# Spectral mixing with a gated feed-forward layer on one core: stores of the gate and up stage issued by GpSimd from the second weight group on

## The chip, the cores and the metric

The kernel runs on one core of one Trainium2 chip. The metric is the device time of one execution in microseconds, the median of several runs. All data is fp32.

## The reference

Two branches work on the same activations x (2 batches of 4096 tokens, width 640) and are mixed by a gate for each token. Cut to what matters:

```python
g = sigmoid((x * gate_w).sum(-1, keepdims=True))

# branch a: a spectral mixer along the 4096 tokens
Xf = rfft2(x, axes=(1, 2))                 # then 4 blocks of 160 channels
hr = relu(zr @ w1[0] - zi @ w1[1] + b1[0]) # complex 2-layer MLP in each block
hi = relu(zi @ w1[0] + zr @ w1[1] + b1[1])
or_, oi_ = ...                             # the same with w2, b2, then soft shrinking by 0.01
a = irfft2(or_ + 1j * oi_, s=(1, 4096))

# branch b: a gated feed-forward layer, hidden width 1728
b = (gelu(x @ w_gate) * (x @ w_up)) @ w_down

out = g * a + (1 - g) * b
```

## The kernel before

The program has three stages that follow each other on TensorE: the gate and up products of branch b (up to about 1380 us), the spectral mixer's middle (up to about 1800 us), and the inverse transform with the down product. The change lies in the first. Every product is made of three matmuls of fp32r parts (high x high, high x low, low x high), and the parts are called forms here: a high part is copied by ScalarE (line 278), the low part subtracted by VectorE (line 281). Products of 2 x 2 blocks are made with seven block products instead of eight, so sums and differences of blocks (t1 to t4 of the activations) get forms too.

**Loops.** The 14 tiles of 128 hidden columns are cut into three weight groups: tiles 0 to 3, 4 to 7 and 8 to 13. For each group the kernel goes over 16 keys, a key being one group and one strip of 512 tokens (two keys make a row couple where a second level of the seven-product scheme joins them: `deep`, strips 3 to 12 in the first two groups). For each key it goes over the group's tiles; one tile of one key is a `quad`. A quad's matmuls are cut into seven steps, and at each step a hook runs what was planned for it: slot 7 x tile + step of that key. `spread(i, s, [f])` plans f for slot s of key i or later. The tables of slots are thus an order written out by hand, and each engine works its instructions in that order.

**Forms of the next key.** `x_prep(nxt, k)` makes form k of the next key: b11, k4, t3, b21, t2, t5, t1, b22, t4 for k = 0 to 8. In the first group t1 to t4 are computed (differences by VectorE, then the form) and kept in device memory by DMAs that GpSimd issues (xD, line 500). From the second group on SyncE loads them instead (line 467), into one of 14 `mid` buffers; the load waits until TensorE has done with what was there.

**Other work in the slots.** From key 14 on the first transform of the spectral mixer runs between quads: `a_load` loads a strip of x (xr, line 790), `a_split` makes its forms xs, `a_step` makes two matmuls a call (line 817) and stores the result as to scr1. In the third group `wd_pre` loads the down weights (draw) and makes seven forms wf for each of seven row pairs, stored in wdf and wdl. In the last key the weights of the spectral MLP are prepared (wm, wl, from raw, rs and rl), partly on GpSimd (lines 884, 885, 904, 912, and line 281 for wm).

**Stores.** A quad ends in h = gelu(gate) * up for 128 hidden columns and 512 tokens, which `h_store` writes to hD, four pieces of 512 bytes for each partition; `half_store` writes half of it. All stores go through `st`, which only lists them; at the end of each quad `flush` issues the listed ones on SyncE's queue, the queue that issues the loads too:

```python
    ld = nc.sync.dma_start
    late = []
    def st(dst, src):
        late.append((dst, src))
    def flush():
        for dst, src in late:
            ld(dst, src)          # line 257
        late.clear()
```

A store waits on SyncE until its source has been made, and what is behind it on that queue waits too. Sources and loaded raw data share 18 `small` buffers; an instruction that takes a buffer next waits until the store that reads it has landed.

The slots of the forms are set here (`z` is 21 in the first two groups, so z + 1, z + 4 and z + 6 are the last of a key's 28 slots; `nxt` is the next key):

```python
            for k, s in enumerate((5, 8, 11, 14, 16, 18, z + 1, z + 4, z + 6) if gr < 2 else
                                  (6, 9, 13, 17, 21, z + 1, z + 2, z + 3, z + 3, z + 5)):
                if k > 5 and deep(key) and not deep(nxt):
                    s += 3
                if k < 9 or nxt[0] == 2:
                    f0, f1, f2_ = x_prep(nxt, k)
                    spread(i, s - 1, [f0])
                    spread(i, s + 1, [f1, f2_])
```

Of the kernel before, what the change touches and what calls it, by code (L numbers as in the profile page):

```python
# [10 lines left out]
F32 = mybir.dt.float32  # L11
# [4 lines left out]
P = 128  # L16
N = 4096
D = 640
# [196 lines left out]
def spectral_mix_kernel(ctx: ExitStack, tc: tile.TileContext, a):  # L215
    nc = tc.nc
    out = a["out"]

    def dr(t, off, ap):
        return bass.AP(tensor=t.tensor, offset=t.offset + off, ap=ap)  # L220
# [7 lines left out]
    def bank():  # L228
        return psum.tile([P, 512], F32, name="bank", tag="bank")
# [13 lines left out]
    def small(shape, dt=F32, name="small"):  # L243
        return pool.tile(shape, dt, name=name, tag="small", bufs=18)
# [6 lines left out]

    def st(dst, src):
        late.append((dst, src))

    def flush():
        for dst, src in late:
            ld(dst, src)
        late.clear()

    scr1 = [dram.tile([32, P, D], F32, name=f"scr1_{b}") for b in range(2)]  # L260
# [3 lines left out]
    hD = dram.tile([64, P, 14 * P], F32, name="hD")  # L264
    wdf = [dram.tile([P, 13 * 320], F32, name=f"wdf_{j}") for j in range(7)]
    wdl = dram.tile([P, 7 * 320], F32, name="wdl")
# [10 lines left out]
    def high(dst, src, scale=1.0):  # L277
        nc.scalar.activation(dst, src, AF.Copy, scale=scale)  # L278
# [4 lines left out]
    def split(dst_h, dst_l, src, eng=nc.vector):  # L283

        high(dst_h, src)
        low(dst_l, src, dst_h, eng)
# [22 lines left out]
    def deep(key):  # L309
        return key[0] < 2 and FIRST <= key[1] < LAST  # L310
# [135 lines left out]
    def x_raw(key, names=("b11", "b21", "b12", "b22", "k4")):  # L446
        d = XT.setdefault(key, {})
        for n in names:
            if (key[0] != 1 or made(key) or n != "b12") and not (key[0] == 1 and deep(key) and n == "b21"):
                r = d[n] = small([P, 512], name="xraw")  # L450
                ld(r, a["xT"][key[1], ("b11", "b21", "b12", "b22", "k4").index(n)])
# [112 lines left out]
                inner.pop()()  # L564

    def h_store(tp, t, h):
        st(dr(hD, 4 * tp * P * 14 * P + t * P, [[14 * P, P], [P * 14 * P, 4], [1, P]]),
           h.rearrange("p (t n) -> p t n", t=4))

    def x_of(o, *names):  # L570
# [11 lines left out]
    def quad(key, t, hook):  # L582
# [65 lines left out]
        def half4():  # L648
            run(C, prod(w["u2"], x_of(o, "t4")), first=False)
            nc.vector.tensor_add(u2, C, u2)  # L650
            nc.vector.tensor_mul(v["h2"], v["h2"], v["u4"])  # L651
            if ahead_:
                half_store(key[1], t, 1, v["h2"])
            elif not dp:
                nc.vector.tensor_mul(v["h"][:, :256], u2, p1)
                h_store(key[1], t, v["h"])
# [18 lines left out]
                q.pop(0)[1]()  # L675

    def half_store(tp, t, q, h):
        st(dr(hD, (4 * tp + 2 * q) * P * 14 * P + t * P, [[14 * P, P], [P * 14 * P, 2], [1, P]]),
           h.rearrange("p (t n) -> p t n", t=2))

    def deep_parts(gr, tp, t):
# [95 lines left out]
    F1, XR, XS, GW = {}, {}, {}, []  # L777
# [28 lines left out]
    def a_step(b, n2, h):  # L806
        xs = XS.pop((b, n2, h))
        m = n2 if n2 < 16 else 32 - n2
        f = F1[m // 5][:, m % 5]
        if h == 0:  # L810
            XS[b, n2] = small([P, D], name="as")
        stg = XS[b, n2]
        hi, lo = (slice(0, 64), slice(64, P))[::1 - 2 * h]
        for q in range(2):
            cs = slice(320 * q, 320 * q + 320)
            pa = bank()
            nc.tensor.matmul(pa[:, :320], f[:, h], xs[:, cs], start=True, stop=True)  # L817
            nc.scalar.activation(stg[hi, cs], pa[lo, :320], AF.Copy)  # L818
            nc.vector.tensor_add(stg[hi, cs], pa[hi, :320], stg[hi, cs])  # L819
        if h:  # L820
            st(dr(scr1[b], n2 * D, [[32 * D, 4], [P * D, 32], [1, D]]), XS.pop((b, n2)))

    def gates(b):
        nc.scalar.activation(gs[:, b, 0], G[:, b], AF.Sigmoid)
# [357 lines left out]
    def wd_raw(t):  # L1182
        raw = RAW["d", t] = small([P, D], name="draw")
        if t < NPAIR:
            ld(raw, a["wd"][t * P:(t + 1) * P])
        else:
            nc.gpsimd.memset(raw[64:], 0.0)
            ld(raw[:64], a["wd"][t * P:])
# [10 lines left out]
    def wd_pre(j):  # L1199
        o = {}  # L1200
        pair = (j, j + 6) if j < 6 else (12, 13)

        def loads():
            for t in pair:
                wd_raw(t)

        def sums(k):
            def f():
                if not o:
                    r1, r2 = (RAW.pop(("d", t)) for t in pair)  # L1210
                    o.update(b11=r1[:, :320], b12=r1[:, 320:], b21=r2[:, :320], b22=r2[:, 320:])
                n, p, q = (("t1", "b12", "b11"), ("t2", "b22", "t1"), ("t3", "b22", "b12"), ("t4", "b21", "t2"))[k]
                if k % 2 == 0:
                    o["x"] = small([P, 2, 320], name="wx")
                o[n] = o["x"][:, k % 2]
                nc.vector.tensor_sub(o[n], o[p], o[q])
            return f

        def form(n):
            def f():  # L1220
                w = small([P, 2, 320], F32R, name="wf")
                p, q = HI[n], LO.get(n, 13)
                wh, wl = (w[:, 0], w[:, 1]) if p < q else (w[:, 1], w[:, 0])
                if j == 6 and n in HALF:
                    x = o[n][:64]
                    nc.gpsimd.memset(wl[64:].bitcast(F32), 0.0)
                    split(wh[:64], wl[:64], x)
                    high(wh[64:], x)
                else:
                    split(wh, wl, o[n])  # L1230
                if n == "b22":
                    st(dr(wdf[j], 320 * p, [[13 * 320, P], [1, 320]]), wh.bitcast(F32))
                    st(dr(wdl, 320 * j, [[7 * 320, P], [1, 320]]), wl.bitcast(F32))
                else:
                    st(dr(wdf[j], 320 * min(p, q), [[13 * 320, P], [320 * abs(q - p), 2], [1, 320]]), w.bitcast(F32))
            return f
        return [loads], [sums(0), sums(1), form("t1"), form("b21")], [sums(2), sums(3), form("t2"), form("b11"),
                                                                      form("t3"), form("t4"), form("b22")]
# [308 lines left out]
    def spread(i, s, fs):  # L1547

        for k, f in enumerate(fs):
            j, q = i, max(s + k, 0)  # L1550
            while j < last and q >= points(j):
                j, q = j + 1, q - points(j)
            slots.setdefault((j, q), []).append(f)
# [6 lines left out]
    for k, (b, n2) in enumerate(a_seq):  # L1560
        i, j = steps_a[k]
# [16 lines left out]
    for i, (gr, tp) in enumerate(keys):  # L1578
        if deep((gr, tp)) and tp % 2:
            p, f = x_deep(gr, tp)  # L1580
# [26 lines left out]
            spread(34 + 2 * j, 1 + 5 * k, [f])  # L1607
    for i, key in enumerate(keys):
        gr, tp = key
        nxt = keys[i + 1] if i < last else None  # L1610
        quads = [t for t in groups[gr] if t < NPAIR]
        nq = len(quads)
        if nxt:
            if not i:
                x_raw(nxt)
            z = 7 * (nq - 1)
            for k, s in enumerate((5, 8, 11, 14, 16, 18, z + 1, z + 4, z + 6) if gr < 2 else
                                  (6, 9, 13, 17, 21, z + 1, z + 2, z + 3, z + 3, z + 5)):
                if k > 5 and deep(key) and not deep(nxt):
                    s += 3  # L1620
                if k < 9 or nxt[0] == 2:
                    f0, f1, f2_ = x_prep(nxt, k)
                    spread(i, s - 1, [f0])
                    spread(i, s + 1, [f1, f2_])
            if gr < 2 and nxt[0] == 2:
                spread(i, z + 7, x_prep(nxt, 9))
        for j, t in enumerate(quads):
            def hook(k):
                for f in slots.get((i, 7 * j + k), ()):
                    f()  # L1630
            (quad if i else plain)(key, t, hook)
            if gr == 2 and j == 1:
                mixed(key)
            if i % 16 == 15:
                WG.pop(t)
            if 0 < i + 1 < last and j == nq - 1:
                x_raw(keys[i + 2])
            n = len(late)
            for f, *args in todo.get((i, j), []):
                f(*args)  # L1640
            new = late[n:]
            del late[n:]
            flush()
            late.extend(new)
        for q in range(7 * nq, 7 * nq + 14) if i == last else ():
            for f in slots.get((i, q), ()):
                f()
        XO.pop(key)
# [13 lines left out]
    for ch in range(1, 2 * NCH):  # L1662
        b, c = chunks[ch]
# [9 lines left out]
    wl = lambda part, *js: [(wd_load, j, part) for j in js]  # L1673
# [13 lines left out]
    for i in range(S + 2):  # L1687
# [18 lines left out]
        if 0 <= i - 1 < S:  # L1706
            b, c, n = steps[i - 1]
# [72 lines left out]
```

## Time and profile before

| | |
|---|---|
| three runs | 2531.83, 2541.38, 2542.81 us; median 2541.38 |
| profiled execution | 2531.49 us, its span 2529.7 us |
| TensorE matmuls, weight loads | busy 2522.0 and 2516.3 us |
| VectorE, ScalarE, GpSimd | busy 2078.9, 1492.6 and 387.3 us |
| SyncE's DMA queue | 445.02 MB, 54.6% of the 16 DMA engines' span |
| GpSimd's DMA queue | 51.00 MB, 5.5% of it |

The span runs from the first to the last instruction; the execution's own time is 1.8 us longer. Rows of the profile name the engine (PE is TensorE, PEld its weight loads, DVE VectorE, ACT ScalarE, POOL GpSimd, SP SyncE; a q marks the queue that issues), the source line, the operation and output<-input without buffer numbers. In a timeline the first column is the start and the second the duration, both in us; in square brackets stands how long the engine was idle before it and what ended that. In a list of waits the numbers are microseconds in total, times, and the longest.

### The profile page before, as it was taken

To read this page: it belongs to the slowest core of one execution; us is meant where nothing else is said; L and a number is where in the kernel's file an instruction comes from. 1 tells how busy PE (TensorE), PEld (TensorE's weight loads), DVE (VectorE), ACT (ScalarE), POOL (GpSimd) and SP (SyncE) were. 2 spreads that over 40 slices of the span, in tenths; PEclk is the share of its full clock that TensorE was granted. 3 is DMA by queue.
4 is the path that set the end of the run, shared out by engine and by line. 5 is a ranking of instruction groups with operands and counts; after the bars stand their busy time and mean duration, and the time that the engine had idled before them with its cause. 6 is when DMAs were issued, how large, how long until landed. Compare 5 with 4: busy or idle time off the path is not lost.

```text
span 2529.7 us, 54653 instructions
## 1 busy us (share of the span) xinstructions
PE 2522.0 (100%) x20239; PEld 2516.3 (99%) x20239; DVE 2078.9 (82%) x4323; ACT 1492.6 (59%) x3503; POOL 387.3 (15%) x404
## 2 busy tenths in 40 slices
PE   9999999999999999999999999999999999999999
PEld 9999999999999999999999999999999999999999
DVE  7677788777777877787668788888999999899998
ACT  5455456656656666666556778787644444444443
POOL 0111100000000000000003111111133333333332
PEclk9999999999999999999999999999999999999999
DMA  6566666777777677777667455548744444444432
GB/s 216 203 214 229 224 224 211 245 234 241 234 251 236 220 235 243 237 239 227 217 228 220 130 164 142 161 144 270 289 142 147 157 157 140 133 152 157 154 131 102
DMA packets 351422, 499.50 MB, mean 197 GB/s; under 512 B 26028, under 2 KB 223276, under 8 KB 351156
## 3 DMA queue, kind: packets, MB, share of 16 engines
q1 hardware_dynamic: 333684, 445.02, 54.6%
q0 software_dynamic: 17472, 51.00, 5.5%
q8 instruction: 159, 2.61, 0.4%
q14 instruction: 107, 0.88, 0.1%
HBM read 307.10 MB, written 188.81 MB: 196 GB/s over the span
## 4 chain that ended last, share of the span: by engine, by line
PE 95%; DVE 2%; DMA 2%; ACT 1%; issue 0%; SPq 0%; DVEq 0%; ACTq 0%
PE bank L562 52%; PE bank L1406 22%; PE bank L297 14%; PE bank L983 3%; PE bank L694 2%; PE bank L817 1%; PE bank L1064 1%; PE bank L1065 1%; DMA xraw<-in_xT_dram 0%; DMA wdf<-wf 0%; PE bank L1066 0%; DMA scr<-as 0%; DMA zl<-zl 0%; DVE xo L281 0%; DMA wx<-wdf 0%
## 5 line engine op out<-in xcount | busy, mean ns | idle before, releaser
L562 PE MATMUL bank<-xo,w 128*128 128x256 f32 x11196 | 1319.4, 277 | 1.6 <-ACT u L588 0.6
L562 PEld LDWEIGHTS bank<-xo,w 128*128 128x128 f32 x11196 | 1298.0, 188 | 3.4 <-ACT u L588 1.2
L1406 PE MATMUL bank<-wx,ho 128*128 128x320 f32 x3844 | 560.7, 306 | 0.0
L1406 PEld LDWEIGHTS bank<-wx,ho 128*128 128x128 f32 x3844 | 557.2, 187 | 0.0
L281 DVE TENSOR_TENSOR ho<-hraw,ho 128x640 fp32r<-128x640 f32 (+3 forms) x384 | 260.8, 720 | 23.1 <-ACT ho L278 20.2
L588 ACT ACTIVATE u<-bank 128x256 f32<-128x256 f32 x328 | 125.5, 383 | 174.6 <-PE bank L562 166.4
L278 ACT ACTIVATE ho<-hraw 128x640 fp32r<-128x640 f32 x320 | 167.1, 571 | 97.7 <-PE bank L1406 74.9
L281 DVE TENSOR_TENSOR xs<-xr,xs 64x640 fp32r<-64x640 f32 x128 | 105.0, 820 | 75.8 <-ACT xs L278 73.6
L640 DVE TENSOR_TENSOR u<-bank,u 128x256 f32<-128x256 f32 x204 | 85.9, 421 | 86.4 <-ACT u L588 85.5
L281 DVE TENSOR_TENSOR xo<-xraw,xo 128x512 fp32r<-128x512 f32 x194 | 133.2, 687 | 16.4 <-ACT xo L278 15.1
L297 PE MATMUL bank<-wm,h 128*128 128x320 f32 (+1 forms) x792 | 137.6, 309 | 0.0
L819 DVE TENSOR_TENSOR as<-bank,as 64x320 f32<-64x320 f32 x256 | 113.9, 484 | 21.8 <-ACT as L818 20.1
L278 ACT ACTIVATE xo<-xraw 128x512 fp32r<-128x512 f32 x194 | 121.6, 627 | 6.1 <-DMA xraw<-in_xT_dram 4.9
L297 PEld LDWEIGHTS bank<-wm,h 128*128 128x128 f32 (+1 forms) x792 | 117.9, 185 | 1.3
L588 ACT ACTIVATE p<-bank 128x256 f32<-128x256 f32 x144 | 55.2, 383 | 105.8 <-DVE h L651 54.6
L562 PE MATMUL bank<-wx,ho 128*128 128x320 f32 x764 | 116.3, 307 | 0.0
L562 PEld LDWEIGHTS bank<-wx,ho 128*128 128x128 f32 x764 | 112.0, 188 | 0.0
L818 ACT ACTIVATE as<-bank 64x320 f32<-64x320 f32 x256 | 96.7, 426 | 23.8 <-PE bank L817 20.3
L278 ACT ACTIVATE xs<-xr 64x640 fp32r<-64x640 f32 x128 | 94.0, 734 | 22.9 <-DMA xr<-in_x_dram 21.1
L278 ACT ACTIVATE ho<-hs 128x640 fp32r<-128x640 f32 (+1 forms) x128 | 68.5, 570 | 61.5 <-DVE ho L281 42.1
L770 POOL MEMSET h<- 64x512 f32 x16 | 8.4, 523 | 624.9 <-PE bank L817 249.1
L1373 ACT ACTIVATE uu<-bank,gs 128x320 f32<-128x320 f32 x120 | 54.7, 524 | 76.5 <-PE bank L297 76.0
(196 smaller groups left out, 3961.8 us busy)
## 6 DMA issues: line engine op xcount, KB each, us to landing
xo<-xD SPq DMA_DIRECT2D x124, 512.0 KB
xraw<-in_xT_dram SPq DMA_DIRECT2D x215, 256.0 KB
hD<-h SPq DMA_DIRECT2D x184, 256.0 KB
hraw<-hD SPq DMA_DIRECT2D x128, 320.0 KB
xD<-xo POOLq DMA_DIRECT2D x64, 512.0 KB, 3.6
sc<-scr SPq DMA_DIRECT2D x65, 320.0 KB
xr<-in_x_dram SPq DMA_DIRECT2D x64, 320.0 KB
scr<-as SPq DMA_DIRECT2D x64, 320.0 KB
```

The costliest lines, as they stand in the source:

```text
L278: nc.scalar.activation(dst, src, AF.Copy, scale=scale)
L281: eng.tensor_sub(dst, src, hi.bitcast(F32))
L297: nc.tensor.matmul(dst, l, r, start=i == 0, stop=i == len(ops) - 1)
L562: nc.tensor.matmul(dst, l, r, start=first and i == 0, stop=i == len(ops) - 1, skip_group_check=True)
L588: copy = lambda d, s_: nc.scalar.activation(d, s_, AF.Copy)
L640: nc.vector.tensor_add(u4, C, u4)
L694: nc.tensor.matmul(acc, l, r, start=first and i == 0, stop=i == 2, skip_group_check=True)
L818: nc.scalar.activation(stg[hi, cs], pa[lo, :320], AF.Copy)
L819: nc.vector.tensor_add(stg[hi, cs], pa[hi, :320], stg[hi, cs])
L983: nc.tensor.matmul(pz[:, kp * P:(kp + 1) * P], SC[b, c, kp][:, o:o + P], ft, start=True, stop=True)
L1373: nc.scalar.activation(uu[n2][:, cs], pe[:, :320], AF.Copy, scale=gs[:, b, 0, n2:n2 + 1])
L1406: nc.tensor.matmul((X, Y)[k], *op, start=n[k] == 0 and not (more and k), stop=n[k] == tot[k] - 1, skip_group_check=True)
```

## The change

From the second weight group on, `h_store`, `half_store`, `a_step` and the weight forms of `wd_pre` call `st_g` instead of `st`. It issues the store at once on GpSimd's queue, at the place where it is called, and no longer at the quad's end on SyncE's. In the first group they go through `st` as before, and so do the stores of the later stages that call `st`. Second, where a key is `deep` and the next one isn't (strip 12 of the first two groups), form k = 4 (t2 of the next key) moves by seven slots, from 16 to 23; forms 6 to 8 are moved by three there as before.

```diff
+    group = [0]
+
+    def st_g(dst, src):
+        if group[0]:
+            nc.gpsimd.dma_start(dst, src)
+        else:
+            st(dst, src)
+
     def h_store(tp, t, h):
-        st(dr(hD, 4 * tp * P * 14 * P + t * P, [[14 * P, P], [P * 14 * P, 4], [1, P]]),
+        st_g(dr(hD, 4 * tp * P * 14 * P + t * P, [[14 * P, P], [P * 14 * P, 4], [1, P]]),
            h.rearrange("p (t n) -> p t n", t=4))
...
         if h:
-            st(dr(scr1[b], n2 * D, [[32 * D, 4], [P * D, 32], [1, D]]), XS.pop((b, n2)))
+            st_g(dr(scr1[b], n2 * D, [[32 * D, 4], [P * D, 32], [1, D]]), XS.pop((b, n2)))
...
                 if n == "b22":
-                    st(dr(wdf[j], 320 * p, [[13 * 320, P], [1, 320]]), wh.bitcast(F32))
-                    st(dr(wdl, 320 * j, [[7 * 320, P], [1, 320]]), wl.bitcast(F32))
+                    st_g(dr(wdf[j], 320 * p, [[13 * 320, P], [1, 320]]), wh.bitcast(F32))
+                    st_g(dr(wdl, 320 * j, [[7 * 320, P], [1, 320]]), wl.bitcast(F32))
...
     for i, key in enumerate(keys):
         gr, tp = key
+        group[0] = gr
...
-                if k > 5 and deep(key) and not deep(nxt):
-                    s += 3
+                if deep(key) and not deep(nxt):
+                    s += {4: 7, 6: 3, 7: 3, 8: 3}.get(k, 0)
```

(`half_store` and the other branch of the weight forms change in the same way.) Eight lines are added above the quads, so line 257 becomes 259, 467 becomes 475, and so on.

SyncE's queue at a couple's end in the second group, before. xo is a form of the next key loaded from xD_13, xr a strip for the first transform, hD, scr1 stores:

```order
L790 DMA xr_10315<-in_x_dram 128x640
L524 DMA xs_10329<-xA_11_117 128x512
L257 DMA hD_104<-h2_10337 128x2x128
L467 DMA xo_10405<-xD_13_101 128x1024
L257 DMA scr1_1_69<-as_10339 4x32x640
L467 DMA xo_10470<-xD_13_101 128x1024
L790 DMA xr_10528<-in_x_dram 128x640
L257 DMA hD_104<-pb_9908 128x2x128
L467 DMA xo_10584<-xD_13_101 128x1024
L451 DMA xraw_10626<-in_xT_dram 128x512
```

The same place now:

```order
L798 DMA xr_10315<-in_x_dram 128x640
L532 DMA xs_10329<-xA_11_117 128x512
L475 DMA xo_10406<-xD_13_101 128x1024
L798 DMA xr_10527<-in_x_dram 128x640
L475 DMA xo_10567<-xD_13_101 128x1024
L475 DMA xo_10584<-xD_13_101 128x1024
L459 DMA xraw_10628<-in_xT_dram 128x512
```

The three stores are gone from between the loads, and the second xo, which is t2, stands behind the xr load instead of ahead of it.

GpSimd's queue in the last key, where it prepares the spectral weights, before (raw, wl: weights; zl2: a constant part of a later operand):

```order
L884 TENSOR_TENSOR raw_19616<-raw_19616 128x128
L885 TENSOR_TENSOR raw_19616<-raw_19616 128x128
L950 MEMSET zl2_19808 64x1024
L951 MEMSET zl2_19808 2x1024
L950 MEMSET zl2_19811 64x1024
L951 MEMSET zl2_19811 2x1024
L904 MEMSET wl_19840 64x2x256
L912 TENSOR_TENSOR wl_19840<-rs_19620,bh_19841 64x2x256
L884 TENSOR_TENSOR raw_19715<-raw_19715 128x128
```

The same place now:

```order
L892 TENSOR_TENSOR raw_19616<-raw_19616 128x128
L893 TENSOR_TENSOR raw_19616<-raw_19616 128x128
L259 DMA hD_104<-h_19780 128x4x128
L958 MEMSET zl2_19809 64x1024
L959 MEMSET zl2_19809 2x1024
L958 MEMSET zl2_19812 64x1024
L959 MEMSET zl2_19812 2x1024
L912 MEMSET wl_19840 64x2x256
L920 TENSOR_TENSOR wl_19840<-rs_19620,bh_19841 64x2x256
L892 TENSOR_TENSOR raw_19715<-raw_19715 128x128
```

A store of h now stands between the first weights and the memsets, so all that follows on GpSimd waits until VectorE has made that h.

GpSimd's queue in the third group, where a couple's weight forms are stored, now (before, GpSimd had nothing here):

```order
L259 DMA hD_104<-h_12673 128x4x128
L259 DMA wdf_0_105<-wf_12713 128x2x320
L259 DMA scr1_0_68<-as_12636 4x32x640
L259 DMA hD_104<-h_12767 128x4x128
L259 DMA wdf_0_105<-wf_12782 128x2x320
L259 DMA scr1_1_69<-as_12798 4x32x640
```

Here six stores that stood on SyncE between loads follow each other, a four-piece h store just ahead of a weight form.

More of the change, by code (lines that the diff above doesn't have):

```diff
@@ L677, in half_store @@
     def half_store(tp, t, q, h):
-        st(dr(hD, (4 * tp + 2 * q) * P * 14 * P + t * P, [[14 * P, P], [P * 14 * P, 2], [1, P]]),
+        st_g(dr(hD, (4 * tp + 2 * q) * P * 14 * P + t * P, [[14 * P, P], [P * 14 * P, 2], [1, P]]),
            h.rearrange("p (t n) -> p t n", t=2))
@@ L1231, in f @@
                 if n == "b22":
-                    st(dr(wdf[j], 320 * p, [[13 * 320, P], [1, 320]]), wh.bitcast(F32))
-                    st(dr(wdl, 320 * j, [[7 * 320, P], [1, 320]]), wl.bitcast(F32))
+                    st_g(dr(wdf[j], 320 * p, [[13 * 320, P], [1, 320]]), wh.bitcast(F32))
+                    st_g(dr(wdl, 320 * j, [[7 * 320, P], [1, 320]]), wl.bitcast(F32))
                 else:
-                    st(dr(wdf[j], 320 * min(p, q), [[13 * 320, P], [320 * abs(q - p), 2], [1, 320]]), w.bitcast(F32))
+                    st_g(dr(wdf[j], 320 * min(p, q), [[13 * 320, P], [320 * abs(q - p), 2], [1, 320]]), w.bitcast(F32))
             return f
```

## The prediction

> **What bounds the kernel now.** I read the page first.
>
> ```profile
> span 2529.7 us, 54653 instructions
> PE 2522.0 (100%) x20239; PEld 2516.3 (99%) x20239; DVE 2078.9 (82%) x4323; ACT 1492.6 (59%) x3503; POOL 387.3 (15%) x404
> PEclk9999999999999999999999999999999999999999
> ```
>
> TensorE is busy for 2522.0 of 2529.7 us, at full clock in every slice. Since a busy TensorE need not be TensorE at its peak, the second view is busy time by stretch. The changed part reaches from the second weight group's start (near 418 us) to the last of the gate and up stage (near 1380 us); the third stretch holds the last row couple's last key, where the next stage is prepared.
>
> ```profile
> core 0: us, PE busy (x) PEld busy (x) DVE busy (x) ACT busy (x) POOL busy (x), PEclk, DMA share, GB/s
> 418.00:800.00 382.00, 381.85 (x3321) 381.06 (x3320) 285.38 (x659) 229.48 (x543) 2.66 (x5) 1.00 0.73 237
> 800.00:1340.00 540.00, 539.60 (x4702) 539.41 (x4702) 405.04 (x918) 340.37 (x803) 11.60 (x23) 1.00 0.73 232
> 1340.00:1380.00 40.00, 39.74 (x344) 39.27 (x343) 35.15 (x83) 24.50 (x73) 23.55 (x31) 1.00 0.80 243
> ```
>
> Over these 962 us TensorE's matmuls are idle for 0.15 + 0.40 + 0.26 = 0.81 us, and its weight loads for 0.94 + 0.59 + 0.73 = 2.26 us. The matmul count per microsecond is the same in the first two stretches (3321 / 382 = 8.69 and 4702 / 540 = 8.71), so no slow feeding hides inside the busy time. **So whatever the change improves here, this execution can give back 0.8 us, and 2.3 us at most.** GpSimd is nearly free until 1340 us (14 of 922 us) and 59% busy after it.
>
> Third, the waits of SyncE's queue and of ScalarE between 410 and 1340 us:
>
> ```profile
> SPq L257 <- DVE h L655: 165.3, 60, 6.7
> SPq L467 <- PE bank L562: 26.8, 40, 8.3
> ACT xs L278 <- DMA xr<-in_x_dram: 21.1, 13, 4.1
> ```
>
> SyncE stands 165 us in 60 stores (line 257) until VectorE has made the h that they store, and the loads queue behind them. ScalarE in turn waits 21 us for xr loads. The longest such wait, in time:
>
> ```profile
> 1136.86 1.05 SPq L790 DMA_DIRECT2D xr<-in_x_dram  x1
> 1143.91 0.74 ACT L278 ACTIVATE xs<-xr 64x640 fp32r<-64x640 f32 x1 [4.07 <-DMA xr<-in_x_dram]
> 1144.68 0.82 DVE L281 TENSOR_TENSOR xs<-xr,xs 64x640 fp32r<-64x640 f32 x1 [5.04 <-ACT xs L278]
> PE bank L562 <- DVE u L640: 0.4, 1, 0.4
> ```
>
> An xr load that was issued late held ScalarE for 4.07 and VectorE for 5.04 us, and TensorE felt 0.4 us of it, its only listed wait in this stretch. Elsewhere the cushion was thick enough.
>
> **The change, part by part.** *Stores off SyncE.* 300 stores leave its queue: 141 of h in four pieces a partition, 40 of half an h in two pieces, 63 of as, 56 of weight forms. SyncE isn't the bound, so this is worth only what late loads cost TensorE now: between 0 and the 0.8 us of matmul idle; I take 0.4, the one wait above.
>
> *Stores on GpSimd.* The trace has DMAs issued by GpSimd, all with one contiguous piece a partition:
>
> ```profile
> L500 POOL DMA_DIRECT2D xD<-xo x64: 531/531/699, 24.6 to 455.6; - x64
> DMA to landing us min/median/max: 2.9/3.6/8.2
> ```
>
> No row has two or four pieces. If pieces cost nothing, a store occupies GpSimd for 0.53 us: 300 x 0.53 = 159 us. If its time goes by pieces, it is 2.12 us for four and 1.06 for two; 21 of the weight forms have two: 141 x 2.12 + 61 x 1.06 + 98 x 0.53 = 416 us, 43% of 962. GpSimd doesn't saturate at either end. I take 1.1 us for the large store, nearer the lower end, since that is the only measured row.
>
> What a slow store can delay is the buffer that it reads. In the changed order, the shortest recurring distance from a producer to the instruction that waits for the store's landing is a weight form whose buffer ScalarE's xs takes next:
>
> ```profile
> 872.27 0.49 DVE L281 TENSOR_TENSOR wf<-draw,wf 128x320 fp32r<-128x320 f32 x1
> 872.79 0.36 SPq L257 DMA_DIRECT2D wdf<-wf  x1
> 879.40 0.74 ACT L278 ACTIVATE xs<-xr 64x640 fp32r<-64x640 f32 x1
> ```
>
> From 872.76 to 879.40 are 6.64 us. The store needs 1.1 us of issue (two pieces, upper end) and 3.6 us to land, counted from its issue on: at most 4.7 us, with 1.9 us over. With a four-piece h store just ahead of it, at its upper end, it is 6.8 us, 0.2 us late. I take no cost.
>
> On this a rule speaks against the change: VectorE can lock GpSimd out while it writes descriptors. The row above says 531 ns as minimum and median of 64 issues and 699 as maximum, beside a VectorE that is busy 82% of the span. The Trainium skill, "SBUF — State Buffer", section "SBUF: two separate sides", states that a DMA issued by GpSimd is starved of descriptors while VectorE runs an operation in a two-port mode. By it each store would start up to one VectorE operation (0.5 us) later, and the distance of 6.64 us would still hold, so the sum is the same by both; the trace shows no starving.
>
> *Order on GpSimd in the last key.* This is where I see a price. GpSimd prepares weights there; now it must first issue the store of an h that VectorE makes at 1346.41.
>
> ```profile
> 1346.41 0.42 DVE L655 TENSOR_TENSOR h<-u,p 128x256 f32<-128x256 f32 x1
> 1343.19 0.98 POOL L950 MEMSET zl<- 64x1024 f32 x1
> 1346.25 0.95 POOL L951 MEMSET zl<- 2x1024 f32 x1
> 1348.78 1.40 POOL L912 TENSOR_TENSOR wl<-rs,bh 64x512 fp32r<-64x512 f32 x1 [1.12 <-ACT bh L278]
> 1350.14 0.46 POOL L884 TENSOR_TENSOR raw<-raw 128x128 f32<-128x128 f32 x1
> 1351.40 0.64 POOL L885 TENSOR_TENSOR raw<-raw 128x128 f32<-128x128 f32 x1
> 1352.57 1.88 ACT L278 ACTIVATE wm<-raw 128x128 fp32r<-128x128 f32 x10
> 1356.56 0.59 ACT L771 ACTIVATE gelu<-bank 64x512 f32<-64x512 f32 x1 [2.11 <-issue]
> ```
>
> Four zl memsets run from 1343.19 to 1347.20 now, ahead of that h. After: h at 1346.83, store 0.53 to 2.12, memsets 4.0, the wl memset 0.5 and wl 1.4, four raw operations 1.9 (1350.14 to 1352.04). That ends at 1355.2 to 1356.8 where it ended at 1352.04. ScalarE's ten wm copies need raw and start 2.6 to 4.2 us after 1352.57. Its 2.11 us of idle ahead of L771 absorb that much; it is 0.5 to 2.1 us late for the bank copies that release TensorE. I take 1.0 us; the bounds are 0 (banks ahead cover it) and 4.2 (nothing does).
>
> *The form made later.* At a couple's end t2 of the next key moves by seven steps, one tile.
>
> ```profile
> 712.10 0.52 SPq L257 DMA_DIRECT2D scr<-as  x1
> 721.60 0.32 SPq L467 DMA_DIRECT2D xo<-xD  x1
> 722.02 0.38 SPq L790 DMA_DIRECT2D xr<-in_x_dram  x1
> ```
>
> In the second group this is the load that holds SyncE from 712.62 to 721.60, for a buffer that TensorE still reads, with an xr load behind it. Moved behind that xr load it waits for a buffer still, so it lands about when it did (0.4 us later for one more issue), and xr goes first. In the first group VectorE and ScalarE do the same four instructions one tile later. I take 0, bounds 0.4 either way.
>
> **Sum.** -0.4 + 0 + 1.0 + 0 = +0.6 us on the profiled execution, which took 2531.49 us (span 2529.7): 2532.1, between -2.3 and +4.6.
>
> The three timed runs gave 2531.83, 2541.38 and 2542.81: the profiled execution is like the fastest, and the median lies 9.9 us above. No view shows where the others lost those 10 us. A late xr load, as at 1136.86, is a candidate: its 5 us of VectorE idle nearly reached TensorE. The change gives exactly these loads more lead, so I hold the lower level the likelier for its median. **Forecast: 2532 us**, which is 0.37% under the median before; about 0.5% is what a measurement of this kernel can tell from no change, so it counts as no change.
>
> **The rivals.** *No effect on the level*: 2541.4 + 0.6 = 2542 us, if the 10 us have nothing to do with SyncE's queue. For it: no row ties them to it. Also no change.
>
> *Slower: stores land too late in the third group.* If GpSimd's stores land as its slowest row (8.2 us) and not as the median, the weight form takes 1.1 + 8.2 = 9.3 us against 6.64: ScalarE stands 2.7 us, once a key, in 16 keys, 43 us. ScalarE is idle 37% (200 of 540 us) there, so some 27 us reach TensorE: 2531.5 + 27 = 2559 us, and at the upper level 2568. It decides from a landing of 5.5 us (6.64 less 1.1) on. For it: DMA engines are 73% busy there, and the pieces are small. Against: the median of 64 is 3.6.
>
> *Faster by over 0.5%*: that is under 2528.7 us. All 2.26 us of weight-load idle gone and no price in the last key: 2531.49 - 2.26 = 2529.2, still short by 0.5 us; it takes the start or the other stages as well. That the change does nothing is excluded: 300 stores stand in another queue in the built order.
>
> **Chances.** Forecast at the lower level 0.46, no effect on the level 0.29, slower 0.17, faster 0.08. Same is 0.46 + 0.29 = 0.75. The range reaches from 2528 (2531.49 less the 2.3 bound, and 1 more for the start) to 2552 (the upper level's 2542.8 with the +4.6 bound, 2547, and into the slower case by the first third of its 27 us from 2543); it leaves out most of the slower case and some of the faster, under 0.2.
>
> **What would show it.** Right: TensorE's idle in 418 to 1340 us stays under 0.6 us; SyncE's wait for h is gone from its list; ScalarE's wait for xr falls well under 21 us; GpSimd's hD stores show under 2.2 us each; ScalarE's wm copies near 1352 us start 2 to 4 us later. Wrong: waits of ScalarE or VectorE for "hD<-h" or "wdf<-wf" of more than a few us in sum, GpSimd issues over 2.2 us, or TensorE waits that recur once a key.

## The result and the profile after

The changed kernel takes 2543.61 us in the median of 19 runs (2538.47 to 2559.43), the kernel before 2531.22 us in 19 runs (2529.70 to 2545.62). The ratio is 1.0048, with a 95% interval of 1.0031 to 1.0066: slower, by about 12 us. The forecast was no change, at 2532 us.

Most runs of both kernels and of the variants stand at one of two levels some 12 us apart (before: 14 of 19 near 2530.8, 5 near 2542.8; after: 14 near 2542.7, 5 near 2556.1), so differences below are given at the lower level, against before's runs of the same comparison, of which four far out (2760 to 7905 us) are left aside.

The profiled execution of the changed kernel took 2539.39 us, 7.9 us more than the profiled one of before. First its page, then busy time in the three stretches that the prediction used.

```profile
span 2537.4 us, 54880 instructions
PE 2526.4 (100%) x20239; PEld 2518.8 (99%) x20239; DVE 2080.8 (82%) x4323; ACT 1492.0 (59%) x3503; POOL 602.1 (24%) x704
```

```profile
418.00:800.00 382.00, 381.84 (x3322) 380.99 (x3321) 286.54 (x659) 229.27 (x544) 80.78 (x111) 1.00 0.72 239
800.00:1340.00 540.00, 538.03 (x4663) 536.25 (x4662) 401.98 (x911) 336.29 (x796) 141.26 (x204) 1.00 0.69 229
1340.00:1380.00 40.00, 38.25 (x325) 37.66 (x324) 29.73 (x78) 22.15 (x67) 21.83 (x31) 1.00 0.76 247
```

The matmul counts say where the time went. In the second weight group nothing changed (3322 against 3321). In the third, 39 of 4702 matmuls are missing, 4.5 us at 8.71 a us. Around the last key, up to 1380 us, 19 more are missing, 2.2 us. GpSimd's busy time rose by 215 us and is far from full, as predicted.

The waits of ScalarE for transfers in the third group, of the changed kernel, show what is new:

```profile
ACT xs L286 <- DMA wdf<-wf: 12.8, 5, 3.8
ACT xs L286 <- DMA xr<-in_x_dram: 9.7, 5, 2.5
ACT xo L286 <- DMA xraw<-in_xT_dram: 7.2, 6, 2.2
ACT xs L286 <- DMA hD<-h: 6.4, 4, 2.3
ACT wf L286 <- DMA scr<-as: 3.7, 3, 1.8
ACT h L597 <- DMA scr<-as: 3.3, 3, 1.7
```

The same list of before has two entries:

```profile
ACT xs L278 <- DMA xr<-in_x_dram: 13.8, 8, 4.1
ACT wf L278 <- DMA wdf<-wf: 1.0, 1, 1.0
```

ScalarE now waits some 26 us for stores to land, where it was 1, and 17 us for loads, where it was 14. SyncE, which stood 130 us for h in this stretch before, now stands 246 us at the xo loads until TensorE frees a buffer: the loads run ahead as far as the buffers let them. At the place that the prediction priced at nothing, the timeline of the changed kernel reads:

```profile
872.71 0.71 POOL L259 DMA_DIRECT2D wdf<-wf  x1
873.04 9.17 SPq L459 DMA_DIRECT2D xraw<-in_xT_dram  x5
880.66 0.74 ACT L286 ACTIVATE xs<-xr 64x640 fp32r<-64x640 f32 x1 [1.92 <-DMA wdf<-wf]
```

and the view of that tile, in the same stretch:

```profile
DMA to landing us min/median/max: 7.9/7.9/7.9
```

The weight form's store is issued at 872.71, at almost the same time as before (872.79), and lands 7.9 us later. By the trace's semaphore events it landed after 4.2 us in the kernel before. ScalarE's xs waits 1.92 us for it. Such a wait stands at 880.66, 955.01, 1028.58, 1101.56 and 1172.91 us: once a row couple. How it reaches TensorE shows at the second:

```profile
955.01 0.74 ACT L286 ACTIVATE xs<-xr 64x640 fp32r<-64x640 f32 x1 [3.81 <-DMA wdf<-wf]
955.77 0.38 ACT L596 ACTIVATE u<-bank 128x256 f32<-128x256 f32 x1
956.21 2.71 PE L570 MATMUL bank<-xo,w 128*128 128x256 f32 x20 [0.37 <-ACT u L596]
```

ScalarE's copy u of a bank stands behind xs, and TensorE waits for that copy. In `third_only`, an experiment below, the same chain holds ScalarE for 4.75 and TensorE for 1.30 us.

Last, the last key. From the list of waits between 1340 and 1400 us:

```profile
POOL hD L259 <- DVE wm L878: 8.0, 3, 4.0
POOL hD L259 <- DVE h L663: 5.2, 3, 2.6
DVE wl L921 <- POOL wl L912: 5.6, 3, 2.7
```

and one instance in the timeline, from GpSimd to TensorE:

```profile
1370.93 0.76 POOL L259 DMA_DIRECT2D hD<-h  x1 [4.03 <-DVE wm L878]
1373.48 0.63 POOL L912 MEMSET wl<- 64x640 f32 x1
1374.14 2.28 DVE L921 SCALAR_TENSOR_TENSOR wl<-bh,sgn,rs 2x640 fp32r<-2x640 f32 x1 [2.71 <-POOL wl L912]
1379.84 0.41 DVE L1001 TENSOR_TENSOR zt<-bank,zt 128x256 f32<-128x256 f32 x1
1380.28 0.42 ACT L286 ACTIVATE zs<-zt 128x256 fp32r<-128x256 f32 x1 [4.77 <-DVE zt L1001]
1380.60 0.37 ACT L596 ACTIVATE p<-bank 128x256 f32<-128x256 f32 x1
1381.02 5.18 PE L570 MATMUL bank<-xo,w 128*128 128x256 f32 x29 [1.92 <-ACT p L596]
```

GpSimd's store of h waits 4.03 us, two operations on wm and a memset stand behind it, and VectorE waits 2.71 us for the memset. What stands behind that on VectorE is late: its addition p from a bank, for which TensorE stands 0.47 us at 1378.14, and zt. ScalarE waits 4.77 us for zt, its copy p of a bank stands behind that, and TensorE, which needs the bank, stands 1.92 us.

### The profile page after: what moved, and what is told of

Read it like the earlier page. It is cut to its first block, busy times and chain, and to the rows that moved or that the text cites. A ratio compares the mean times of both kernels' runs of the same rounds, so it can differ in the third digit from the quotient of the medians.

```text
span 2537.4 us, 54880 instructions
## 1 busy us (share of the span) xinstructions
PE 2526.4 (100%) x20239; PEld 2518.8 (99%) x20239; DVE 2080.8 (82%) x4323; ACT 1492.0 (59%) x3503; POOL 602.1 (24%) x704
## 4 chain that ended last, share of the span: by engine, by line
PE 84%; DMA 5%; issue 4%; DVE 4%; POOL 1%; ACT 1%; SPq 0%; POOLq 0%; DVEq 0%; ACTq 0%
PE bank L570 41%; PE bank L1414 22%; PE bank L305 14%; PE bank L991 3%; PE bank L702 2%; DMA scr<-as 1%; DMA xr<-in_x_dram 1%; PE bank L825 1%; DMA hD<-h 1%; DMA wdf<-wf 1%; POOL hD L259 1%; PE bank L1072 1%; PE bank L1073 1%; DVE xo L289 0%; DMA xraw<-in_xT_dram 0%
## 5 line engine op out<-in xcount | busy, mean ns | idle before, releaser
L259 POOL DMA_DIRECT2D hD<-h x161 | 121.7, 756 | 501.4 <-DVE h L663 343.5
L286 ACT ACTIVATE xo<-xraw 128x512 fp32r<-128x512 f32 x194 | 121.6, 627 | 11.9 <-DMA xraw<-in_xT_dram 10.8
L289 POOL TENSOR_TENSOR ys<-y,ys 128x640 fp32r<-128x640 f32 x29 | 45.7, 1575 | 311.1 <-ACT ys L286 274.9
L508 POOL DMA_DIRECT2D xD<-xo x64 | 34.3, 536 | 315.7 <-DVE xo L289 248.8
```

Source lines behind the costliest of these rows:

```text
L259: nc.gpsimd.dma_start(dst, src)
L289: eng.tensor_sub(dst, src, hi.bitcast(F32))
```

## The experiments

Two theories stood at the start: the loss is the late landing of stores in the third group plus GpSimd's order in the last key, or only one of the two; and the form made later was a rival for each. Each edit is made to the changed kernel, whose lines are those with -; the moved form stays in all of them.

**One part at a time.** `t2_only`: no store moves, only the form does.

```
-        group[0] = gr
+        group[0] = 0
```

> All stores on SyncE as before; only t2 is made later. Theory (late store landings and GpSimd's order cost the time): within 2 us of before, ScalarE's waits for stores between 800 and 1340 us stay under 1 us. Rival (the moved form costs it, for example because the load of t2 lands late at the couple's end): 6 to 12 us above before, TensorE's lag arising near 720 us.

Measured: ratio 1.0008 (0.9988 to 1.0028), 1.0 us below before at the lower level (2530.3 against 2531.3). No cost of the moved form shows.

`second_only`: GpSimd stores in the second group alone.

```
-        group[0] = gr
+        group[0] = gr == 1
```

> GpSimd issues the stores in the second weight group alone, t2 moved. Theory: within 2 us of before, since 418 to 800 us lost nothing in the trace of the changed kernel (3322 matmuls against 3321). Rival (any store on GpSimd costs in proportion to their number, 84 of 300): about 3 us slower.

Measured: ratio 0.9992 (0.9971 to 1.0013), 1.1 us below before at the lower level. In the second group no cost of the stores shows on either queue.

`third_only`: the third group without its last key.

```
-        group[0] = gr
+        group[0] = gr == 2 and i < last
```

> GpSimd issues the stores in the third group without its last key, t2 moved. Theory: 4 to 8 us slower than before (6.1 us of lag arose between 738 and 1110 us in the changed kernel), with waits of ScalarE for wdf, scr and hD stores recurring once a row couple, some 25 us in all; nothing lost after 1340 us. Rival (the last key's order carries it all, as the prediction has it): under 1 us slower.

Measured: ratio 1.0050 (1.0028 to 1.0071), 9.9 us above before at the lower level (2541.2), more than expected. The stretch from 800 to 1340 us by windows:

```profile
800.00:1340.00 540.00, 534.16 (x4621) 531.60 (x4620) 399.87 (x905) 332.98 (x787) 138.41 (x200) 1.00 0.68 227
```

and ScalarE's main waits for stores in it:

```profile
ACT xs L286 <- DMA wdf<-wf: 15.0, 5, 4.8
ACT xs L286 <- DMA hD<-h: 8.5, 4, 2.6
ACT wf L286 <- DMA scr<-as: 5.5, 4, 1.7
ACT h L597 <- DMA scr<-as: 4.1, 2, 3.1
```

81 matmuls are missing, 9.3 us; from 1340 to 1380 us none (348). This is most of the loss.

`last_only`: the last key alone.

```
-        group[0] = gr
+        group[0] = i == last
```

> GpSimd issues the stores of the last key alone, t2 moved. Theory: 3 to 5 us slower than before (3.8 us of lag arose between 1364 and 1385 us in the changed kernel), VectorE waiting some 5 us for GpSimd's wl and a TensorE stall near 1376 us. Prediction's step: 1.0 us, at most 4.2. Rival (that stall needs the late landings ahead of it): 0.

Measured: ratio 1.0014 (0.9996 to 1.0032), 2.7 us above before at the lower level (2534.0). The stall is there without any late landing ahead of it:

```profile
1380.39 2.27 DVE L921 SCALAR_TENSOR_TENSOR wl<-bh,sgn,rs 2x640 fp32r<-2x640 f32 x1 [2.71 <-POOL wl L912]
1387.26 0.96 PE L570 MATMUL bank<-xo,w 128*128 128x256 f32 x6 [1.92 <-ACT p L596]
```

The parts add up: -1.1 + 9.9 + 2.7 = 11.5 us, against 11.9 for the whole change.

**The last key, with the stores later.** `last_late`: as `last_only`, with the stores kept on a list and issued by GpSimd at the quad's end.

```
+        for dst, src in late_g:
+            nc.gpsimd.dma_start(dst, src)
+        late_g.clear()
```

> GpSimd issues the stores of the last key alone, but from a list at the quad's end, so that no prepared weight stands behind an h that isn't made yet. Theory (the last key's loss is GpSimd standing for h with wl behind it): the 2.8 us of the run with the last key alone fall under 1 us; VectorE's wait for GpSimd's wl falls from several us to under 2 and TensorE's stall near 1376 us is gone. Rival (the 0.76 us that each store occupies GpSimd, or its landing, makes the loss): 2 to 3 us stay.

Measured: ratio 1.0010 (0.9991 to 1.0030), 2.3 us above before at the lower level. The expected fall under 1 us did not come, because the edit did not do enough: VectorE's wait for wl fell from 5.6 to 2.1 us, but a store still stands ahead of the weights' later half and still waits:

```profile
1365.50 0.77 POOL L269 DMA_DIRECT2D hD<-h  x1 [2.10 <-DVE wm L882]
1367.90 2.27 DVE L925 SCALAR_TENSOR_TENSOR wl<-bh,sgn,rs 2x640 fp32r<-2x640 f32 x1 [1.89 <-POOL wl L916]
1375.28 1.30 PE L574 MATMUL bank<-xo,w 128*128 128x256 f32 x9 [1.92 <-ACT p L600]
```

So it tells nothing about the 0.76 us of an issue. What removes the stall is taking these stores off GpSimd, as in `third_only`.

**Why the third group loses.** Four runs divide the 9.9 us. They, and the runs on queues after them, move stores in the third group without its last key, as `third_only`. `tick3`: as `third_only`, but each store also leaves one of 4 bytes for SyncE.

```
             nc.gpsimd.dma_start(dst, src)
+            k = ticks[0] = ticks[0] + 1
+            st(dr(tickD, 4 * k, [[4, 1], [1, 1]]), flat(src)[:1, :1])
```

> Third group without its last key: the stores go by GpSimd as in the changed kernel, but each also leaves a store of 4 bytes of the same source on SyncE at the quad's end, so that SyncE stands and issues its loads as it did before. Theory A (the loads, no longer held by stores, run ahead and share the DMA engines with the stores that must land): the 10 us of loss fall to under 3, the median landing of xo and xraw loads returns from 7.8 to 5.5 and from 8.0 to 6.7 us, that of wdf stores to under 5.5. Theory B (a store by GpSimd lands later of itself): still 8 to 11 us slower than before, wdf landing stays at 6.5 or more.

Measured: ratio 1.0025 (1.0011 to 1.0038), 3.4 us above before at the lower level (9 of 12 runs, spread from 2531.5 to 2541.6, so this figure is rough). By the trace's semaphore events the xo loads land after 6.0 us in the median, but the xraw loads after 10.0 and the wdf stores after 5.9. The stretch from 800 to 1340 us:

```profile
800.00:1340.00 540.00, 539.48 (x4694) 538.90 (x4693) 404.65 (x918) 339.40 (x801) 141.30 (x205) 1.00 0.71 231
```

ScalarE's main waits for stores in it:

```profile
ACT xs L293 <- DMA wdf<-wf: 10.6, 5, 2.8
ACT xs L293 <- DMA hD<-h: 1.8, 2, 1.4
```

Neither theory had this: holding SyncE back gives 6.5 of the 9.9 us back, though the wdf store near 872 us lands after 8.6 us even so. Theory A's time (under 3) is the nearer one, but the landings that it expected did not come; whether the rest is theory B is tested with `all_pool3` below.

`h_sync3`: h stored by SyncE, as and the weight forms by GpSimd. `h_only3`: the other way round.

```
-        st_g(dr(hD, 4 * tp * P * 14 * P + t * P, ...
+        st(dr(hD, 4 * tp * P * 14 * P + t * P, ...
```

> Third group without its last key: h is stored by SyncE at the quad's end as before, only as and the weight forms by GpSimd. Theory A: SyncE is held by h again, loads come as before, loss under 3 us although 83 stores go by GpSimd. Theory B: the waits for wdf and scr stores stay (some 20 of the 30 us of ScalarE's waits), loss 5 us or more.

> Third group without its last key: only h by GpSimd, as and the weight forms by SyncE at the quad's end. Theory A: SyncE isn't held for h any more, loads run ahead, loss 5 us or more, with waits for wdf<-wf though these go by SyncE. Theory B: only the waits for hD<-h stay (some 8 us of ScalarE's), loss under 4 us.

Measured: 1.0028 (1.0015 to 1.0041) and 1.0022 (1.0014 to 1.0031), both 6.3 us above before at the lower level (in `h_only3` all 11 runs). In `h_only3` no wait for wdf shows, so theory A's reading of it is wrong; the waits are for h, and the longest, 5.09 us, falls on wf near 1342 us. In its profile 22 matmuls are missing from 800 to 1340 us and 35 in the 40 us after, where TensorE stands 2.49 us at 1344.01. Either half of the stores on another queue than the rest costs 6 us; the two do not add up to 9.9. In `h_sync3` the waits for wdf and scr stay (24 us), as theory B says, and neither theory holds in both runs.

`once3`: all stores at once, but on SyncE.

```
-            nc.gpsimd.dma_start(dst, src)
+            ld(dst, src)
```

> Third group without its last key: every store issued at once, at the place of its call, but on SyncE. It parts the place from the engine. Both theories: SyncE stands for each h longer than at the quad's end, loads come late, so waits for xr and xraw grow over the 6 of before; the waits for wdf, scr and hD stores stay under 2 us in sum. If those store waits show here too with 5 us or more, the place of the store, and not GpSimd, makes them.

Measured: ratio 1.0043 (1.0026 to 1.0059), 12.0 us above before (5 runs, 2539.77 to 2546.36). ScalarE waits 50.2 us for xraw and xr loads, and 9.7 us for stores, over the 5 of the expectation, so that this run by itself would lay part of the loss on the place; `gp_late3` below tests that. Here most of the waiting is for loads: a store that is issued at once on SyncE waits there for its source, and the loads behind it wait too.

**Which queue.** `wd_act3`: only the weight forms' stores move, to ScalarE's own queue, at the quad's end.

```
+        for dst, src in late_w:
+            nc.scalar.dma_start(dst, src)
```

> Third group without its last key: the weight forms' stores are issued by ScalarE at the quad's end, on a hardware queue of its own; everything else by SyncE as before. Theory Q (a store on another queue than the loads shares the DMA engines with a burst of loads, where on SyncE's queue it lands ahead of them): the wdf store near 872 us lands after 7 to 9 us as it did by GpSimd (8.5 to 8.7), not after 4.1 to 4.2, the median over 800 to 1340 us is 5.5 or more, and ScalarE waits for wdf<-wf recur once a couple. Rival S (GpSimd's software queue is slow of itself): it lands after 4 to 5 us, median 4.4, and no such wait shows.

Measured: ratio 1.0064 (1.0039 to 1.0089). The matching wdf store lands after 6.5 us, the median is 5.4: between the two theories, and no wait for wdf shows, against theory Q. The loss is another: ScalarE stands at these issues until VectorE has made the form (2.3 us ahead of one at 886.99), and TensorE waits 8.0 us in seven waits for VectorE's as, so its time can't be compared. The runs that decide are the next two.

`all_pool3`: loads and stores together on GpSimd, in SyncE's old order.

```
+    def ld(dst, src):
+        (nc.gpsimd if group[0] else nc.sync).dma_start(dst, src)
...
     def st_g(dst, src):
-        if group[0]:
-            nc.gpsimd.dma_start(dst, src)
-        else:
-            st(dst, src)
+        st(dst, src)
```

> Third group without its last key: all loads and stores that SyncE issues there, in its order of before (stores from the list at the quad's end), are issued by GpSimd instead, so that there is one queue again, with each store ahead of the loads that follow it. Theory Q (a store is late because it shares the DMA engines with loads of another queue): the wdf store near 872 us lands after 4 to 5.5 us, median of wdf under 5.2, ScalarE's waits for wdf and hD stores are under 3 us in sum, and the time is within 5 us of before (GpSimd's issues take some 0.7 us instead of 0.4, which may cost a little through the loads). Rival S (GpSimd's queue is slow in a crowd of itself): landing 7 us or more at the same place, median 6 or more, waits for wdf<-wf once a couple, 8 us or more slower.

Measured: ratio 0.9999 (0.9985 to 1.0013), 1.3 us above before at the lower level (11 of 12 runs, spread from 2530.0 to 2538.7; the profile is of the slowest of these, which lost 30 matmuls from 418 to 800 us, where no store is moved). The stretch from 800 to 1340 us:

```profile
800.00:1340.00 540.00, 539.24 (x4686) 538.06 (x4685) 405.51 (x922) 340.14 (x801) 236.98 (x383) 1.00 0.69 229
```

All of ScalarE's waits for transfers there over 1 us:

```profile
ACT xs L284 <- DMA xr<-in_x_dram: 23.9, 10, 3.9
ACT wf L284 <- DMA scr<-as: 3.7, 3, 2.5
```

The waits for wdf and hD are gone and the loss of time with them, with every store issued by GpSimd. The landing is not as theory Q has it: the store issued at 877.87 lands after 7.4 us, and the median of wdf is 5.5. The issues of GpSimd cost nothing to speak of, although it is busy 237 of 540 us there.

This run and `third_only` differ in two things, the split and the place. `gp_late3` is the control: GpSimd's stores from a list at the quad's end, loads on SyncE.

```
-            nc.gpsimd.dma_start(dst, src)
+            late_g.append((dst, src))
```

> Third group without its last key: stores by GpSimd, but from the list at the quad's end, loads by SyncE. It is the control between the run with the third group alone (GpSimd at once, two queues: 9.9 us slower) and the run with loads and stores together on GpSimd (list at the quad's end, one queue: 1.3 us slower), which differ in two things. Theory (the split into two queues makes the loss): 7 to 13 us slower than before, with ScalarE's waits for wdf, hD and scr stores of 20 us or more between 800 and 1340 us. Rival (the place, at once instead of at the quad's end, makes it): under 3 us slower and waits for stores under 6 us.

Measured: ratio 1.0036 (1.0018 to 1.0054), 9.6 us above before at the lower level (2540.9 against 2531.2), with the loss in the same stretch:

```profile
800.00:1340.00 540.00, 535.50 (x4608) 533.01 (x4607) 400.23 (x902) 331.40 (x785) 136.59 (x197) 1.00 0.69 228
```

and ScalarE's waits for stores back:

```profile
ACT xs L290 <- DMA wdf<-wf: 14.4, 5, 3.6
ACT xs L290 <- DMA hD<-h: 9.6, 4, 3.3
ACT wf L290 <- DMA scr<-as: 5.5, 3, 1.9
```

So neither the place nor the engine that issues the stores makes this loss: **with loads and stores in two queues it is there, 9.6 us; in one queue it is not, 1.3 us.** The larger part is that the loads no longer stand behind the stores: `tick3`, with two queues but with SyncE held, loses 3.4. What the split does is seen in the trace's records of the DMA packets. KB begun in each microsecond at the weight form's store, by packet size, before (all SyncE's) and in `third_only` (the stores GpSimd's, the loads SyncE's):

```
us    before:  h   wdf  scr,xr loads    third_only: h   wdf+scr  loads
             512B 1280B 2560B 4K,2K                4K   5120B    4K,2K
873           146     5   100     0                60     65       44
874            68   221    55    16                92     40       92
875            30    66     0   140                40     25      128
876             0    28     0   184                28     80      164
877             0     0     0   298                28    155      170
878             0     0     0   344                 8    135      216
879             0     0     0   332                 4    125      250
880             0     0     0   358                80     75      170
```

On one queue the 320 KB of wdf are through by 877, and the loads behind them follow. On two, stores and loads go side by side from 873 to 880, and both end late. The Trainium skill, "DMA: Bandwidth & Descriptors", section "Queues, rings and completion order", states that each DMA engine takes turns between the queues for which it has work, a packet at a time. The right half of the table, where bytes of both queues begin in every microsecond, agrees with it. The landing by itself does not decide, though: the medians of h and scr are 5.9 and 9.1 us in `third_only`, 5.9 and 9.0 in `tick3`, 4.8 and 8.7 in `all_pool3`, while ScalarE's waits for stores fall from 35 to 16 and 4 us and the loss from 9.9 to 3.4 and 1.3. Where loads stand behind the stores, ScalarE waits more for loads (24 us for xr in `all_pool3`) and may so reach the buffers after they are free; that is argued, not shown. What stays open too is how much of the 7.4 us in `all_pool3` belongs to GpSimd's queue and how much to the stores ahead of it.

**The two levels.** `rhythm`: a matmul of zeros once a key in the first group, t2 moved, stores on SyncE.

```
+        if key[0] == 0 and t == 1:
+            nc.tensor.matmul(C[:64, :64], zc, zc, start=False, stop=True, skip_group_check=True)
```

> Stores all on SyncE, t2 moved, and in the first weight group one matmul of 64x64 zeros a key, added into a bank that is being summed. It is about the 11 us between the two levels: in every profile at the upper level matmuls of the first group stand 117.8 ns apart from about 60 to 350 us and 113.3 ns in the others, with TensorE never idle. Theory (a rhythm of weight loads and matmuls that lasts until something breaks it): the break restores 113.3 ns at some keys, times spread between the levels, 2531 to 2538, and fewer runs stand at 2541 to 2545. Rival (a clock or the chip's state sets it): two levels 11 us apart as before, in 3 to 5 runs of 10 the upper.

Measured: ratio 1.0000 (0.9980 to 1.0021); 8 of 12 runs from 2530.43 to 2535.25, 4 from 2542.98 to 2547.74. It looks like the rival, and with 12 runs it does not tell the two apart. What sets the level stays open.

No variant beats the kernel before: `second_only` and `t2_only` are 1 us below it, inside their intervals.

## Why the prediction was wrong, step by step

- **The level.** I took the lower of the two levels for the median, and 14 of 19 runs of either kernel stand at their lower one: right, by luck, since two of the three times that I had were at the upper one and the reason was wrong. I held late xr loads for a candidate; some 11 us of the difference lie in the first weight group, where no store is moved. From 100 to 300 us, a profile of the lower level (before) and one of the upper (`t2_only`):

```profile
100.00:300.00 200.00, 200.00 (x1767) 200.00 (x1766) 146.93 (x336) 101.77 (x254) 28.28 (x53) 1.00 0.65 226
100.00:300.00 200.00, 200.00 (x1700) 200.00 (x1699) 142.88 (x323) 97.16 (x243) 27.77 (x52) 1.00 0.61 215
```

  TensorE is busy throughout and its granted clock is 1.00 in both, yet it makes 67 matmuls fewer in 200 us: one each 117.8 ns instead of 113.3, from some 60 to some 350 us. That the changed kernel's median lies inside the range of 2528 to 2552 us is luck as well: the range reaches that far because it spans the upper level, and 2543.6 us is a loss of 12 us at the lower one.
- **Stores off SyncE, -0.4 us.** SyncE's wait for h at its stores is gone from its list, as predicted, and ScalarE's wait for xr fell from 13.8 to 9.7 us in the third group. TensorE gained nothing there, since other waits came; in the second group `second_only` is 1.1 us below before, inside the interval.
- **The issue, 1.1 us for a large store.** The groups of instructions of the changed kernel from 410 to 1340 us give

```profile
L259 POOL DMA_DIRECT2D hD<-h x152 | 114.9, 756 | 456.7 <-DVE h L663 310.9 <-DVE h L659 60.4 <-DVE h L667 26.1
L259 POOL DMA_DIRECT2D scr<-as x63 | 46.0, 730 | 127.0 <-DVE as L827 123.2 <-issue 3.7
```

  or 0.76 and 0.73 us: nearer the row of 0.53, as I took it, and not by pieces. (I put one VectorE operation at 0.5 us; xs takes 0.82 there, and nothing hangs on it.)
- **The landing, 3.6 us, so no cost: this is the step that failed.** I took the median of the xD stores, which were issued in the first group. In the third group the changed kernel's list of DMA issues says

```profile
hD<-h POOLq DMA_DIRECT2D x91, 256.0 KB, 5.6
wdf<-wf POOLq DMA_DIRECT2D x42, 320.0 KB, 5.2
scr<-as POOLq DMA_DIRECT2D x37, 320.0 KB, 9.0
```

  and 7.9 us at the very pair of 6.64 us that I worked out. The late landing is not GpSimd's alone: its quickest wdf store in this stretch lands after 2.4 us, SyncE's quickest before after 2.2. The cost that I put at nothing is 9.9 us (`third_only`). I priced the landing as a property of the issuing engine and did not ask what else would be in flight, and that the same change lets SyncE's loads start while the stores are still under way. The rival that named late landings, deciding from 5.5 us on, had the right mechanism, at a chance of 0.17 and at near three times the price.
- **The rival's price.** I counted a wait for wdf of 2.7 us in each of 16 keys; there are 5, of 2.6 us in the mean. And I let 27 of 43 us of ScalarE's waits reach TensorE. In `third_only` ScalarE waits 49 us for transfers against 15 before, and TensorE loses 9.3: 27% of the increase got through, not 63%. In the profile of the changed kernel it is 16% (4.5 of 29).
- **GpSimd's order in the last key, +1.0 us, bounds 0 and 4.2.** The mechanism is right and the size was not: 2.7 us by itself. I looked at the raw operations and ScalarE's wm copies, which did start late (ScalarE waits 1.9 us for raw), but the way to TensorE went through VectorE, at wl, because a bank's addition and zt stand behind that wait, and ScalarE's copy of a bank behind zt. The store of each later quad repeats it; I counted one.
- **The form made later, 0.** Nothing in `t2_only` speaks against it.

## What to carry to other kernels

Moving stores to another engine's queue to free the loads is not a change of issue time only: it takes away the order of stores ahead of loads, and the buffers that the stores read come free later. Price a store's landing with what will be in flight beside it then, from rows of the same stretch, not by the issuing engine's median elsewhere. On an engine that works in order, a store that waits for its source is a wait of everything behind it: follow it to the engine that waits for the last of these.

## What the runs showed of the hardware that was not expected

The same stream of matmuls can run at two paces 4% apart, one each 117.8 or 113.3 ns, with TensorE always busy and its granted clock at 1.00. The slower pace lasts for some 290 us, which makes some 11 us (2460 matmuls at 4.5 ns): most of the difference of the two levels.

A stall of TensorE may cost more than its length. After the 1.92 us stall at 1381 us in the changed kernel the clock fell, and matmuls stood 213 ns apart until some 1384.9 us:

```profile
1378.00:1382.00 4.00, 1.95 (x12) 1.75 (x13) 3.52 (x8) 1.72 (x4) 2.55 (x4) 0.94 0.65 246
1382.00:1386.00 4.00, 4.00 (x25) 4.00 (x24) 3.77 (x7) 1.56 (x5) 2.08 (x2) 0.63 0.00 0
```

In `last_only` and `last_late` the same stall was not followed by it. The Trainium skill, "TensorE: Matmul & The Clock Gate", section "Why this matters for your kernels", warns of gaps of over about 3 us; here 1.92 us, with 0.47 us shortly ahead of it, was enough once in three. Of all nine stalls of 1.7 to 2.5 us that TensorE has in these traces from 60 to 1800 us, four are followed by such a stretch (the others in `gp_late3`, `h_sync3` and `h_only3`). The length alone does not decide: 1.76 us in `gp_late3` was enough, and 2.41 us in `once3`, at 1324.58, was not.
